# A state-space scan feeding a gated FFN: two sequences of the first scan, and w_in's first piece, ahead of the others

## The chip, the cores and the metric

The kernel runs on one core of one Trainium2 chip. The metric is the device time of one execution in microseconds; of the kernel before, six runs are given by their median, lowest and highest. A profile is one profiled execution; its rows are in microseconds from the start of its span unless marked ns. The engines are PE (TensorE matmul) with PEld (its weight loads), DVE (VectorE), ACT (ScalarE), POOL (GpSimd) and SP (SyncE, which here only issues DMAs).

## The reference

Four sequences of 768 positions with 8 heads go through a chunked state-space scan; its output, as 3072 tokens of 256, goes through `h @ w_in`, a gate with a cosine, and `@ w_out` (256 to 2048 and back).

```python
for c in range(nc):                        # chunks of 32
    cum = np.cumsum(la, axis=-1)           # la = log(clip(a))
    L = np.exp(cum[..., :, None] - cum[..., None, :]) * causal
    M = np.einsum('bhin,bhjn->bhij', Cc, Bc) * L
    y[:, :, sl] = M @ xc + (Cc @ state) * exp(cum)
    state = decay_full * state + sum(Bx)
h = x @ w_in;  g = h * np.cos(h);  out = g @ w_out
```

The weights arrive as 64-bit floats; x, a, B and C are 32-bit.

## The kernel before

The kernel takes six chunks of 128 positions (NC = 6) of all four sequences (NB = 4). For each chunk it makes yT (the scan's output, transposed, 512 tokens), and then 16 steps of the FFN (NF = 16, `n` counts them over all chunks). Step n is `first(n)`: four matmuls hp = w_in x yT, an integer copy k on ScalarE and w = hp/2pi - k on VectorE; `gate(n)`: the sine on ScalarE; `gated(n)`: gT = hp x w on VectorE; and, two steps later (LAG = 2), `second(n - 2)`: o += gT x w_out. In the first chunk the steps alternate between the halves of the tokens: even n takes sequences 0 and 1, odd n sequences 2 and 3 (`turn_of`), so hp(0) needs yT of the first two sequences only.

The order of each engine's instructions is the order in which the program writes them: there is a manual schedule, and each engine takes its own in turn. What the first chunk does for sequence b:

- `spread_a(b)` (L294): matmuls that spread a into PSUM (a_ps); `decays0(b)` (L303): a scan on VectorE over it (L309), then a copy and a memset on GpSimd (L312, L313), which give lam, the decays within halves of 64.
- `cross(b)` (L315): one matmul (L318) for two sequences, the product of the decays between the halves; two ScalarE copies put it into lam (L321), and `weigh` (L324) scales B by it on GpSimd, for the state (sc).
- `turn(b)` (L354): two TensorE transposes of B and C (L360), and three ScalarE copies to cT and bT.
- `intra(b)` (L369): four matmuls g = B x C (L374), and two VectorE products m = g x lam (L381).
- `finish(b)` (L385): eight matmuls y = m x x (L391), and a ScalarE copy into yT (L395). With `fills=1` it first issues a matmul of ones (L101), whose product isn't used.
- `first_scan` (L720): finish(3), then the 16 matmuls of the state's sums (s_ps, L478).

A weight piece (256 columns of w_in or 256 rows of w_out; 8 of each) comes as 64-bit words and is made 32-bit in pieces. `grade` (L178): ScalarE takes the high words' magnitude (L193), GpSimd clips it (L194), ScalarE scales the low words (L191); with `later=True` the L191 is returned as a function that the caller runs later. `join` (L201): VectorE shifts and merges bits (L207, L209), GpSimd adds the low words and writes the piece (L217). hp(0) and hp(1) use w_in's first piece, hp(2) and hp(3) its second; the second matmuls of steps 0 and 1 use w_out's first.

PSUM is given out in rings of two: tag "h" (hp, and before it a_ps and tp), tag "o" (o, and before it the warm-up, l_ps and y), tag "scan" (pairs of banks: g, tp, s_ps). A tile waits until the readers of the one two places before it in its ring are done. The same holds for the rings of SBUF tiles (m has four).

The SP queue issues the loads in the order in which the program writes them: `load(0, b)` for each sequence (B, C, x), with w_in's first piece ahead of the fourth sequence (L219 to L222), then a as rows (L223), five weight pieces, and, behind the writes of a_cut and a_all to DRAM (L691), the rest of the weights and the loads of chunk 1 (`rest_of_loads`).

Of the kernel before, what the change touches and what calls it, by code (L numbers as in the profile page):

```python
# [25 lines left out]
def kernel(  # L26
# [59 lines left out]
    def bank(shape, name, tag):  # L86
        return psum.tile(shape, FP32, tag=tag, bufs=2, name=name)

    def pair(name):

        return psum.tile([P, 2, 4 * P], FP32, tag="scan", bufs=2, name=name)
# [86 lines left out]
    def grade(which, i, later=False, n=1):  # L178

        t = words.pop((which, i), None)
        if t is None:
            return
        mag = conv.tile([P, 2 * WC], FP32, tag="mag", bufs=3, name="mag")
        last = conv.tile([P, 2 * WC], U32, tag="last", bufs=3, name="last")
        low, high, mags, lasts = (shares(which, ap, n) for ap in (t[:, :, 0], t[:, :, 1], mag, last))
        held[which, i] = list(zip(high, shares(which, mag.bitcast(U32), n), lasts))

        def rest(e=0):  # L190
            ACT.activation(lasts[e], low[e], AF.Copy, scale=2.0 ** -29)  # L191
        for e in range(n):
            ACT.activation(mags[e], high[e].bitcast(FP32), AF.Abs)  # L193
            G.tensor_scalar(out=mags[e], in0=mags[e], scalar1=MOST, scalar2=LEAST,  # L194
                            op0=ALU.min, op1=ALU.max)
            if not later:
                rest(e)
        if later:
            return rest
# [17 lines left out]
            G.tensor_tensor(out=dst.bitcast(U32), in0=bits, in1=last, op=ALU.add)  # L217

    for b in range(NB):  # L219
        if b == NB - 1:  # L220
            fetch("in", 0)
        load(0, (b, b + 1))  # L222
    nc.sync.dma_start(  # L223
# [70 lines left out]
    def spread_a(b, tag):  # L294


        spread[b] = ps = bank([P, H, W], "a_ps", tag)
        for t in range(2):
            PE.matmul(ps[t * W:(t + 1) * W], lhsT=those[:, b:b + 1].to_broadcast([P, W]),  # L299
                      rhs=a0s[:, t], start=True, stop=True, tile_position=(0, t * W),  # L300
                      skip_group_check=True)

    def decays0(b):  # L303

        lam[0, b] = l = scan.tile([P, 2, H, W], FP32, tag="lam", bufs=4, name="lam")
        flat = "p h i -> p (h i)"
        V.tensor_tensor_scan(out=l[:, 0].rearrange(flat), data0=spread.pop(b).rearrange(flat),  # L309
                             data1=unit0.rearrange(flat), initial=0.0,  # L310
                             op0=ALU.mult, op1=ALU.add)
        G.tensor_copy(out=l[W:P, 1], in_=l[W:P, 0])  # L312
        G.memset(l[W:P, 0], 0.0)  # L313

    def cross(b, tag):  # L315

        ps = bank([P, H, W], "l_ps", tag)
        PE.matmul(ps, lhsT=fros[:, b:b + 2].rearrange("p b j -> p (b j)"), rhs=tos,  # L318
                  start=True, stop=True)
        for t in range(2):  # L320
            ACT.copy(out=lam[0, b + t][0:W, 1], in_=ps[t * W:(t + 1) * W])  # L321
            weigh(0, b + t)

    def weigh(c, b):  # L324

        scaled[c, b] = sc = scan.tile([P, H, N], FP32, tag="sc", bufs=NB, name="sc")
        l = lam[c, b][:, :, P - 1:P] if c > 0 else lam[c, b][:, 1, :, W - 1:W]
        G.tensor_tensor(out=sc, in0=raw[c][0][:, 0, heads(b)],  # L328
                        in1=l.to_broadcast([P, H, N]), op=ALU.mult)
# [21 lines left out]
            return  # L351
        weigh(c, b)

    def turn(b, tag=None):  # L354

        bc = raw[0][0]
        tp = (pair("tp")[:, 0] if tag is None else bank([P, 4 * P], "tp", tag)
              ).rearrange("p (k i) -> p k i", k=4)
        for k in range(2):
            PE.transpose(tp[:, k], bc[:, k, heads(b)].rearrange("p h n -> p (h n)"), ident)  # L360

        cT = scan.tile([P, 2, P], FP32, tag="cT", name="cT")
        for t in range(2):
            ACT.activation(cT[:, t], tp[:, 1], AF.Copy, scale=slot[:, t:t + 1])
        bT = scan.tile([P, P], FP32, tag="bT", name="bT")
        ACT.copy(out=bT, in_=tp[:, 0])
        part[0, b] = (bT, cT)

    def intra(b):  # L369
        bT, cT = part[0, b]  # L370
        g = [pair("g") for _ in range(2)]
        for q in range(4):
            r = slice(32 * q, 32 * q + 32)
            PE.matmul(g[q // 2][:, q % 2, 0:2 * P], lhsT=bT[r],  # L374
                      rhs=cT[r].rearrange("p t (s i) -> p s t i", s=2), start=True, stop=True)
        l = lam.pop((0, b))
        m = scan.tile([P, 2, H, W], FP32, tag="m", bufs=4, name="m")
        for q in range(2):
            of = [t[:, :, q * HH:(q + 1) * HH].rearrange("p s (k t) i -> p k s (t i)", k=2)
                  for t in (m, l)]  # L380
            V.tensor_tensor(out=of[0], in0=g[q][:, :, 0:2 * P].rearrange(  # L381
                "p k (s i) -> p k s i", s=2), in1=of[1], op=ALU.mult)
        part[0, b] = m
# [122 lines left out]
        c, f = divmod(n, NF)  # L506
        return (f % 2, f // 2) if c == 0 else divmod(f, NJ)

    def first(n):
        c, f = divmod(n, NF)  # L510
        hp[n] = bank([P, TB], "hp", "h")

        u, j = turn_of(n)
        to_ = hp[n].rearrange("p (e t s i) -> p e t s i", e=2, t=2, s=2)
        y = yT[c].rearrange("p k (u s t i) -> p k u t s i", u=2, s=2, t=2)
        for e in range(2):
            fs = slice((2 * j + e) * P, (2 * j + e + 1) * P)
            for k in range(KT):
                PE.matmul(to_[:, e], lhsT=w_in[:, k, fs], rhs=y[:, k, u],  # L519
                          start=(k == 0), stop=(k == KT - 1), skip_group_check=True)  # L520

        k = ffn.tile([P, TB], I32, tag="k", name="k")
        ACT.activation(k, hp[n], AF.Copy, bias=0.25, scale=INV_2PI)  # L523
        turns[n] = w = ffn.tile([P, TB], FP32, tag="w", name="w")
        V.scalar_tensor_tensor(out=w, in0=hp[n], scalar=INV_2PI, in1=k,  # L525
                               op0=ALU.mult, op1=ALU.subtract)
# [137 lines left out]
    warm = bank([P, 4, P], "warm", "o")  # L664
    fill(warm, 2)
    spread_a(0, "h")
    turn(0)
    spread_a(1, "h")
    spread_a(2, "o")
    spread_a(3, "h")  # L670
    for b in range(NB):
        decays0(b)
    turn(1, "h")
    cross(0, "o")
    intra(0)
    turn(2, "h")
    cross(2, "o")
    intra(1)
    finish(0, "o")
    grade("in", 0, n=2)  # L680
    intra(2)
    turn(3, "h")
    finish(1, "o", 1)

    la = const.tile([RB, NU, P], FP32, name="la")
    cut = const.tile([RB, NU, P], FP32, name="cut")
# [4 lines left out]
        nc.sync.dma_start(  # L691
            out=dst.rearrange("(u b) h (c p) -> (b h c) u p", u=NU, p=P), in_=src)

    join("in", 0)
    finish(2, "o")
    intra(3)
    grade("in", 1)
    rest = grade("out", 0, later=True)
    join("in", 1)


    piece = {n: ("in", (n + 3) // 2) if n % 2 else ("out", n // 2) for n in range(NF)}
# [16 lines left out]

    def first_scan():  # L720

        finish(3, "o")
        for u in range(2):
            sums[u] = pair("s_ps")[:, :, 0:2 * D]
            for t in range(2):
                sum_up(0, 2 * u + t, sums[u][:, t])
# [25 lines left out]
    def ends(n):  # L752
        return [(c, us) for c, at, us, _, _, end in plan if at + end == n]

    rest_of_loads()
    for n in range(NC * NF + LAG):
        c, f = divmod(n, NF)
        if n < NC * NF:
            if f == 0 and c > 0:
                load(c + 2)  # L760
            first(n)
            if n == 0:
                first_scan()
            for at in pairs(n):
                turn2(*at)
            rests = [rest] if n == 0 else []
            if n + 1 in piece:
                rests.append(grade(*piece[n + 1], later=True))
            gate(n)
            for rest in rests:  # L770
                if rest:
                    rest()
            if n in piece:
                join(*piece[n])

            behind = [lambda at=at: halved(*at) for at in halves_at(n)]
            behind = [lambda at=(c, 2 * u + 1): masked(*at) for c, u in pairs(n - 2)] + behind
            if n not in piece and behind:
                behind.pop(0)()
            gated(n)  # L780
            for do in behind:
                do()
            if n in (1, 2):
                carry(0, n - 1, sums[n - 1])
        for i, js in differ_at.get(n, ()):
            differ_w(i, js)
        if n >= LAG:
            second(n - LAG)
        for c, u in pairs(n - 1):
            intra2(c, u)  # L790
            masked(c, 2 * u)
        for c, us in ends(n):
            finish2(c, us)
            if 1 in us:
                raw.pop(c)
        for c, u in pairs(n + 1):
            for b in (2 * u, 2 * u + 1):
                reaches(c, b)
                load_along(c + 1, (b,))
# [30 lines left out]
```

## Time and profile before

| what | us |
|---|---|
| median of 6 runs (lowest, highest) | 382.77 (382.22, 383.33) |
| the profiled execution, its own time | 382.64 |
| its span | 380.8 |
| TensorE busy / weight loads busy | 374.0 / 330.6 |
| VectorE / GpSimd / ScalarE busy | 279.8 / 213.0 / 172.6 |
| granted TensorE clock | 1.00 |

How to read it: the page of a profile gives busy times, the span in 40 slices, the chain of work that ended last, and groups of instructions; a group's row is line, engine, operation, out<-in with the shapes and the count, then busy time and mean ns, then the idle time of the engine just before it and what ended that. The timeline merges neighbouring instructions of one kind into a row of start, duration, engine, line, operation and count; a matmul of 32-bit data is two passes, so four matmuls of hp are x8. Two VectorE or ScalarE instructions in a row overlap by some 0.1 us. Shares of DMA over the first stretches: 0.99 from 4 to 10 us, 1.01 from 10 to 14, 0.95 from 14 to 18, 1.00 from 18 to 21.5, 1.08 from 21.5 to 25, 0.92 from 25 to 60.

### The profile page before, as it was taken

How to read it: one execution, taken by the hardware profiler on the slowest of the kernel's cores; microseconds unless marked ns; L12 is line 12 of the kernel's file. 1: busy time of each engine (PE TensorE's matmuls, PEld its weight loads, DVE VectorE, ACT ScalarE, POOL GpSimd, SP SyncE). 2: the span in 40 equal slices, each digit the busy share in tenths (PEclk: the TensorE clock that was granted, in tenths of full speed). 3: DMA queues.
4: the chain of work that ended last, by engine and by line, in shares of the span. 5: the costliest groups of instructions: out<-in, count | busy, mean ns of one | idle time of the engine just before them, and what ended most of it. 6: DMA issues, size and time to landing. Idle time of an engine off the chain costs nothing.

```text
span 380.8 us, 7676 instructions
## 1 busy us (share of the span) xinstructions
PE 374.0 (98%) x2980; PEld 330.6 (87%) x2980; DVE 279.8 (73%) x431; ACT 172.6 (45%) x303; POOL 213.0 (56%) x330
## 2 busy tenths in 40 slices
PE   8989999999999999999999999999999999999995
PEld 2568888889989899998899998899998999999995
DVE  8898999789699748877648976756976862644643
ACT  3887666544334433443434453424444433433441
POOL 5776555479863436773544683543585343454451
PEclk9999999999999999999999999999999999999999
DMA  7989999859322861420941340100100100000101
GB/s 86 261 238 279 248 223 138 151 88 171 90 87 77 111 60 58 134 75 2 109 46 55 83 116 10 43 2 2 28 3 3 28 2 2 12 17 0 29 0 28
DMA packets 106371, 30.41 MB, mean 80 GB/s; under 512 B 75521, under 2 KB 102241, under 8 KB 106337
## 3 DMA queue, kind: packets, MB, share of 16 engines
q1 hardware_dynamic: 106176, 29.81, 39.3%
q8 instruction: 23, 0.38, 0.4%
q10 hardware_dynamic: 160, 0.13, 0.1%
q14 instruction: 12, 0.09, 0.1%
HBM read 26.59 MB, written 3.34 MB: 79 GB/s over the span
## 4 chain that ended last, share of the span: by engine, by line
PE 96%; DVE 2%; POOL 0%; issue 0%; POOLq 0%
PE hp L519 44%; PE o L616 33%; PE o L578 7%; PE g L423 3%; PE y L457 3%; PE y L450 1%; PE tp L406 1%; PE a_ps L299 1%; PE warm L101 1%; DVE mag L209 1%; PE g L374 1%; DVE mag L207 1%; PE o L655 1%; PE s_ps L478 0%; PE l_ps L318 0%; PE tp L360 0%
## 5 line engine op out<-in xcount | busy, mean ns | idle before, releaser
L519 PE MATMUL hp<-yT,w_in 128*128 128x256 f32 x768 | 184.0, 382 | 1.7 <-DVE gT L535 1.3
L519 PEld LDWEIGHTS hp<-yT,w_in 128*128 128x128 f32 x768 | 139.4, 190 | 22.8 <-issue 4.9
L560 POOL TENSOR_TENSOR gd<-gT 128x256 f32<-128x256 f32 x79 | 59.4, 752 | 103.4 <-DVE gT L535 74.3
L530 ACT ACTIVATE w<-w,quarter 128x512 f32<-128x512 f32 x96 | 69.3, 722 | 84.4 <-DVE w L525 84.4
L525 DVE SCALAR_TENSOR_TENSOR w<-hp,k 128x512 f32<-128x512 f32 x96 | 65.6, 684 | 53.0 <-ACT k L523 52.9
L523 ACT ACTIVATE k<-hp 128x512 int32<-128x512 f32 x96 | 57.1, 595 | 98.3 <-PE hp L519 98.3
L535 DVE TENSOR_TENSOR gT<-hp,w 128x512 f32<-128x512 f32 x96 | 65.1, 678 | 30.6 <-ACT w L530 28.0
L616 PE MATMUL o<-words,gd 128*128 128x128 f32 x474 | 66.9, 277 | 0.0
L616 PEld LDWEIGHTS o<-words,gd 128*128 128x128 f32 x474 | 59.8, 192 | 0.5
L345 DVE TENSOR_TENSOR_SCAN lam<-arow,unit 128x512 f32<-128x512 f32 x40 | 55.8, 1395 | 0.0
L616 PEld LDWEIGHTS o<-w_out,gT 128*128 128x128 f32 x316 | 46.9, 191 | 3.6
L563 POOL TENSOR_TENSOR gd<-gT,gd 128x128 f32<-128x128 f32 x79 | 46.0, 583 | 6.2
L616 PE MATMUL o<-w_out,gT 128*128 128x128 f32 x316 | 48.0, 274 | 0.0
L562 POOL TENSOR_TENSOR gd<-gT,gd 128x128 f32<-128x128 f32 x79 | 42.7, 540 | 6.2
L616 PE MATMUL o<-w_out,gd 128*128 128x128 f32 x158 | 30.6, 275 | 0.0
L616 PE MATMUL o<-words,gT 128*128 128x128 f32 x158 | 30.6, 275 | 0.0
L578 PE MATMUL o<-w_out,gT 128*128 128x256 f32 x128 | 30.2, 379 | 0.0
L578 PEld LDWEIGHTS o<-w_out,gT 128*128 128x128 f32 x128 | 24.2, 190 | 3.3
L436 DVE TENSOR_TENSOR m<-g,lam 128x512 f32<-128x512 f32 x40 | 25.6, 680 | 0.0
L616 PEld LDWEIGHTS o<-words,gT 128*128 128x128 f32 x158 | 24.0, 192 | 0.0
L616 PEld LDWEIGHTS o<-w_out,gd 128*128 128x128 f32 x158 | 24.0, 192 | 0.0
L328 POOL TENSOR_TENSOR sc<-bc,lam 128x128 f32<-128x128 f32 x20 | 8.3, 417 | 14.4 <-DVE lam L345 7.3
(91 smaller groups left out, 291.4 us busy)
## 6 DMA issues: line engine op xcount, KB each, us to landing
arow<-a_cut SPq DMA_DIRECT2D x20, 512.0 KB, 3.9
words<-in_moe_w_in_dram SPq DMA_DIRECT2D x8, 512.0 KB, 6.0
words<-in_moe_w_out_dram SPq DMA_DIRECT2D x8, 512.0 KB, 8.8
out_dram<-sum SPq DMA_DIRECT2D x18, 128.0 KB, 2.5
xr<-in_x_dram SPq DMA_DIRECT2D x4, 512.0 KB
along<-a_all SPq DMA_DIRECT2D x20, 64.0 KB
xr<-in_x_dram SPq DMA_DIRECT2D x8, 128.0 KB
bc<-in_B_dram SPq DMA_DIRECT2D x4, 256.0 KB, 5.1
```

The source lines that it names most:

```text
L345: V.tensor_tensor_scan(out=lam[c, b][:, hs].rearrange("p h i -> p (h i)"), data0=rows_.rearrange("p h i -> p (h i)"), data1=unit.rearrange ...
L436: V.tensor_tensor(out=of[0], in0=g[q][:, :, s * 2 * P:(s + 1) * 2 * P], in1=of[1], op=ALU.mult)
L519: PE.matmul(to_[:, e], lhsT=w_in[:, k, fs], rhs=y[:, k, u], start=(k == 0), stop=(k == KT - 1), skip_group_check=True)
L523: ACT.activation(k, hp[n], AF.Copy, bias=0.25, scale=INV_2PI)
L525: V.scalar_tensor_tensor(out=w, in0=hp[n], scalar=INV_2PI, in1=k, op0=ALU.mult, op1=ALU.subtract)
L530: ACT.activation(cos, cos, AF.Sin, bias=quarter, scale=TWO_PI)
L535: V.tensor_tensor(out=gT[n], in0=hp.pop(n), in1=cos, op=ALU.mult)
L560: G.tensor_tensor(out=d[:, 0:2], in0=g[:, 1:2].to_broadcast([P, 2, P]), in1=g[:, 3::-3], op=ALU.subtract)
L562: G.tensor_tensor(out=d[:, 2], in0=g[:, 0], in1=d[:, 0], op=ALU.subtract)
L563: G.tensor_tensor(out=d[:, 3], in0=g[:, 2], in1=d[:, 2], op=ALU.subtract)
L578: PE.matmul(o[c, u][:, t], lhsT=g[:, 2 * e + t], rhs=w_out[:, 2 * j + e], start=(j == e == t == 0), stop=(j == NJ - 1 and e == 1), skip_gr ...
L616: PE.matmul(at[q], lhsT=a_[q], rhs=w[q], start=(j == 0 and q in starts), stop=(j == NJ - 1), skip_group_check=True)
```

## The change

Only the start of the kernel changes, up to the end of step 0, and with it the places of a few steps in the queues.

- On SP, w_in's first piece is fetched ahead of the third sequence instead of the fourth.
- The first two sequences are scanned first: cross(0), intra(0), turn(1), grade of w_in's first piece, then the third's a, decays and intra(1), cross(2), the fourth's a. `decays0(3)` is split: its tile is allocated early, so that cross(2)'s copies can write it, and its scan comes behind the join of w_in's first piece. finish(0) and finish(1) follow each other; the filling matmul is gone.
- `weigh` is no longer part of `cross`: those of sequences 0 and 1 come behind a_cut and a_all on GpSimd, those of 2 and 3 in `start`.
- hp(0) is issued before sequences 2 and 3 are finished: its first half, then the turn of the fourth sequence, then its second half, then intra(3), and only then step 0's k and w; finish(2) and finish(3) follow, then gate(0).
- The ScalarE work on the low words (L191) of w_in's second piece, w_out's first and w_in's third comes behind gate(0) in a row; the joins of w_in's second and w_out's first piece surround gated(0). Before, the L191 of w_in's second piece followed its L193 directly.
- The sums of the state (s_ps) come behind hp(1) instead of ahead of it.
- The tiles of `turn` are half as large (two of 128 columns) and come from tags "h" and "o".

```diff
     for b in range(NB):
-        if b == NB - 1:
+        if b == 2:
             fetch("in", 0)
         load(0, (b, b + 1))
...
-    def decays0(b):
+    def decays0(b, early=False):
...
+        if early:
+            lam[0, b] = scan.tile([P, 2, H, W], FP32, tag="lam", bufs=4, name="lam")
+            return
...
     def cross(b, tag):
...
-        for t in range(2):
-            ACT.copy(out=lam[0, b + t][0:W, 1], in_=ps[t * W:(t + 1) * W])
-            weigh(0, b + t)
+        crosses.update({b + t: ps[t * W:(t + 1) * W] for t in range(2)})
+
+    def crossed(b):
+        ACT.copy(out=lam[0, b][0:W, 1], in_=crosses.pop(b))
...
-    def first(n):
+    def first(n, between=None):
...
         for e in range(2):
+            if e and between:
+                between()
...
+        if not between:
+            turned(n)
+
+    def turned(n):
...
     spread_a(0, "h")
-    turn(0)
+    turn(0, pair("tp")[:, 0, 0:2 * P])
     spread_a(1, "h")
+    decays0(0)
+    decays0(1)
+    cross(0, "o")
+    crossed(0)
+    crossed(1)
+    intra(0)
+    turn(1, bank([P, 2 * P], "tp", "h"))
+    grade("in", 0, n=2)
     spread_a(2, "o")
+    decays0(2)
+    intra(1)
+    cross(2, "o")
     spread_a(3, "h")
-    for b in range(NB):
-        decays0(b)
-    turn(1, "h")
-    cross(0, "o")
-    intra(0)
-    turn(2, "h")
-    cross(2, "o")
-    intra(1)
+    decays0(3, early=True)
+    crossed(2)
+    crossed(3)
     finish(0, "o")
-    grade("in", 0, n=2)
+    finish(1, "o")
+    join("in", 0)
+    decays0(3)
+    turn(2, bank([P, 2 * P], "tp", "h"))
     intra(2)
-    turn(3, "h")
-    finish(1, "o", 1)
...
-    join("in", 0)
-    finish(2, "o")
-    intra(3)
-    grade("in", 1)
-    rest = grade("out", 0, later=True)
-    join("in", 1)
+    weigh(0, 0)
+    weigh(0, 1)
...
     def first_scan():
 
-        finish(3, "o")
...
+    def start():
+
+        first(0, lambda: turn(3, bank([P, 2 * P], "tp", "o")))
+        intra(3)
+        turned(0)
+        later = [grade("in", 1, later=True)]
+        finish(2, "o")
+        for b in range(NB):
+            if b > 1:
+                weigh(0, b)
+            del lam[0, b]
+        finish(3, "o")
+        later.append(grade("out", 0, later=True))
+        gate(0)
+        for do in (*later, grade(*piece[1], later=True)):
+            if do:
+                do()
+        join("in", 1)
+        gated(0)
+        join("out", 0)
+
     rest_of_loads()
+    start()
...
+            if n == 0:
+                continue
             first(n)
-            if n == 0:
+            if n == 1:
                 first_scan()
```

More of the change, by code (lines that the diff above doesn't have):

```diff
@@ L301, in spread_a @@
                       skip_group_check=True)
-    def decays0(b):
-        lam[0, b] = l = scan.tile([P, 2, H, W], FP32, tag="lam", bufs=4, name="lam")
+    def decays0(b, early=False):
+        if early:
+            lam[0, b] = scan.tile([P, 2, H, W], FP32, tag="lam", bufs=4, name="lam")
+            return
+        if (0, b) not in lam:
+            decays0(b, True)
+        l = lam[0, b]
         flat = "p h i -> p (h i)"
@@ L313, in decays0 @@
         G.memset(l[W:P, 0], 0.0)
+    crosses = {}
     def cross(b, tag):
@@ L352, in decays, with turn @@
         weigh(c, b)
-    def turn(b, tag=None):
+    def turn(b, tp):
         bc = raw[0][0]
-        tp = (pair("tp")[:, 0] if tag is None else bank([P, 4 * P], "tp", tag)
-              ).rearrange("p (k i) -> p k i", k=4)
+        tp = tp.rearrange("p (k i) -> p k i", k=2)
         for k in range(2):
@@ L375, in intra @@
                       rhs=cT[r].rearrange("p t (s i) -> p s t i", s=2), start=True, stop=True)
-        l = lam.pop((0, b))
+        l = lam[0, b]
         m = scan.tile([P, 2, H, W], FP32, tag="m", bufs=4, name="m")
@@ L765 @@
                 turn2(*at)
-            rests = [rest] if n == 0 else []
-            if n + 1 in piece:
-                rests.append(grade(*piece[n + 1], later=True))
+            rests = [grade(*piece[n + 1], later=True)] if n + 1 in piece else []
             gate(n)
```

## The prediction

> **What bounds the kernel now.** I read first the page's chain of work, then the idle times of TensorE's groups, then its timeline over the first 32 us, and last the timelines of ScalarE, VectorE and GpSimd over the same stretch.
>
> ```profile
> PE 96%; DVE 2%; POOL 0%; issue 0%; POOLq 0%
> ...
> L519 PE MATMUL hp<-yT,w_in 128*128 128x256 f32 x768 | 184.0, 382 | 1.7 <-DVE gT L535 1.3
> ```
>
> TensorE ends the kernel. Its largest group waited 1.7 us in all, 1.3 of them once, for a gT. Where that was, the timeline tells:
>
> ```profile
> 18.18 2.29 PE L519 MATMUL hp<-yT,w_in 128*128 128x256 f32 x8 [0.31 <-POOL w_in L217]
> 20.40 0.64 PE L391 MATMUL y<-m,xr 128*32 128x128 f32 x16
> 20.86 0.63 PE L478 MATMUL s_ps<-xr,sc 128*32 128x64 f32 x32
> 21.54 1.99 PE L519 MATMUL hp<-yT,w_in 128*128 128x256 f32 x8
> 24.87 1.97 PE L519 MATMUL hp<-yT,w_in 128*128 128x256 f32 x8 [1.34 <-DVE gT L535]
> 26.68 1.89 PE L578 MATMUL o<-w_out,gT 128*128 128x256 f32 x8
> ```
>
> hp(0) starts at 18.18, hp(1) at 21.54, hp(2) at 24.87; from there no row of TensorE shows idle time, and the table of stretches gives it 35.00 of 35.00 us between 25 and 60. What follows hp(2) is the same work before and after the change. So the whole question is **when hp(2) starts**: later or earlier by d, the kernel ends later or earlier by d, unless a new wait follows.
>
> hp(2) needs three things: its PSUM bank (gT(0) of VectorE), w_in's second piece (the sum at L217 on GpSimd), and TensorE free. The rows that prepare that piece:
>
> ```profile
> 18.51 0.68 ACT L191 ACTIVATE last<-words 128x512 uint32<-128x512 uint32 x1
> ...
> 21.12 0.37 ACT L395 COPY yT<-y 128x256 f32<-128x256 f32 x1
> 21.38 0.68 ACT L193 ACTIVATE mag<-words 128x512 f32<-128x512 f32 x1
> 22.10 0.72 ACT L530 ACTIVATE w<-w,quarter 128x512 f32<-128x512 f32 x1
> 22.73 1.25 ACT L191 ACTIVATE last<-words 128x512 uint32<-128x512 uint32 x2
> ```
>
> ```profile
> 20.48 0.98 DVE L209 SCALAR_TENSOR_TENSOR mag<-words,mag 128x512 uint32<-128x512 uint32 x1
> 21.39 0.68 DVE L525 SCALAR_TENSOR_TENSOR w<-hp,k 128x512 f32<-128x512 f32 x1
> 21.99 1.12 DVE L207 TENSOR_SCALAR mag<-mag 128x512 uint32<-128x512 uint32 x1
> ```
>
> ```profile
> 21.55 1.28 POOL L217 TENSOR_TENSOR w_in<-mag,last 128x512 uint32<-128x512 uint32 x1 [0.63 <-DVE mag L209]
> 22.79 0.79 POOL L194 TENSOR_SCALAR mag<-mag 128x512 f32<-128x512 f32 x1
> ```
>
> Before, the low words of that piece are ready at 19.19 (the L191 at 18.51) and the piece at 22.83, two us ahead of hp(2). Only gT(0) is late.
>
> **What the Trainium skill says.** "SBUF — State Buffer", section "Who interferes with whom": VectorE and GpSimd share a port pair under an exclusive lock; a VectorE instruction in a two-port mode, or with two SBUF inputs, and a GpSimd instruction that reads SBUF exclude each other for the whole instruction. The trace agrees: L207 of 21.99 ends 0.29 after GpSimd's L217 lets go (22.82), and took 1.12 where an undisturbed one takes 0.41; L209 of 20.48 ends 0.55 after GpSimd's L194 ends (20.92). "TensorE: Matmul & The Clock Gate", section "What's actually happening": full clock needs sustained work, and an idle window of about 3.4 us halves it. Here a 64-row pass of a_ps took 0.9 us at 4.8 and 0.43 from 6.6 on, and the gap of 1.34 us left hp(2) at full speed; longer gaps the trace doesn't show.
>
> **The change part by part.** I worked out the start of each instruction in the new order as the later of its engine's last issue and its last input, with the durations above and those of the same rows elsewhere in the first 25 us, and the lock. The same rule on the old order puts hp(2) at 24.60 where the trace has 24.87, so it is good to some 0.3 us.
>
> *Sequences 0 and 1 ahead.* The first cross product follows a_ps(1): 7.50 instead of 9.59. The decays' copies end at 9.74, m(0) at 10.67 (was 12.75), m(1) at 13.05 (was 14.66), with the third scan (1.22) between them on VectorE. y(1) takes the bank of the second cross product, so it waits for its two copies (0.58 each), to 13.61; yT(1) is done at 14.67.
>
> *w_in's first piece ahead of sequence 2 on SP.* Landings of before are 10.27 for sequence 2's x and 12.26 for the piece, so the piece takes 2.0 and now lands near 10.25; sequence 2's loads land 2.0 later, 11.0 to 12.3. Their first user (the turn of 2) comes at 14.05, which hides it with 2.4 to spare; without that cover it would cost up to 2.0. The piece is joined at 15.7 (was 19.29).
>
> *hp(0).* The turn of 2 is at 14.05, its ScalarE copies (0.80) stand behind yT(1), g(2) is at 15.53, hp(0)'s first half at 16.2, the turn of 3 at 17.2, hp(0) done at 18.7 instead of 20.47. That is 1.8 us won.
>
> *But hp(1) needs sequences 2 and 3.* The turn of 3 lies inside hp(0); its copies end at 18.45, g(3) at 19.24, m(3) (0.2 of hand-over, 0.61 + 0.69) at 20.72, y(3) at 21.21, yT(3) runs 21.25 to 21.62. Before it ran 21.12 to 21.49. So hp(1) starts at 21.68 against 21.54: **the gain is gone** already. The four s_ps (0.62) now stand behind hp(1) and end at 24.04.
>
> *The low words of w_in's second piece move.* This edit decides. ScalarE's L191 for that piece, at 18.51 before, now stands behind gate(0), that is behind yT(3), the high words of w_out's first piece, the sine, and the high words of w_in's third: 21.25 + 0.27 + 0.57 + 0.63 + 0.57 = 23.29, done 23.97. Three L191 in a row follow each other there, with k(1) queued behind (25.0; was 23.89). On GpSimd the joining sum (L217) also stands behind L194 of w_in's third piece, which waits for ScalarE until 23.49. Then the lock: L207 of w_out's first piece (from 23.46, behind gT(0)) holds it to 23.87, L194 ends 0.47 later at 24.34, L209, waiting since 23.90, holds it to 24.88, and L217 ends 1.14 later, at **26.02**. hp(2) starts at **26.07**.
>
> *The rest.* Four L328 moved later end at 21.4, before s_ps needs them (23.4). The filler of 0.53 removed from y(1)'s bank lies where TensorE would now wait anyway. a_cut and a_all are issued some 1.3 later (before: 16.67 and 17.36), and the SP queue behind them too (w_out's third piece, chunk 1's loads): before, a_cut landed only at 23.89, behind weight pieces that keep the DMA engines at 1.0 of their time from 18 to 25, so this lies in that queue; uncovered it would be 1.3 on loads whose users come 4 us later or more. Allocating the fourth decays early and the smaller tp tiles: the same instructions, 0.
>
> *What is late next.* hp(3) needs gT(1). k(1) 25.0, w at 25.65, L207 waits for w_out's sum (1.28 behind 26.02: 27.27) until 27.55, L194 to 28.02, L209 to 28.57, gT(1) 29.18, usable 29.31; hp(3) is due at 26.07 + 3.46 = 29.53. That holds by 0.2.
>
> **Sum.** 26.07 - 24.87 = +1.20 us. On the profiled execution, 382.64 (span 380.8 and 1.8 around it), that is 383.84; its time is 0.13 below the median of 382.77, so in medians **384.0**. Unknown from both sides: who gets the lock. If L217 goes before L209, hp(2) is at 25.73 (+0.86); if L194 also goes before L207 (they are 0.03 apart), 25.57 (+0.70). If the rule is as early here as on the old order, +1.47.
>
> **The rivals.** 0.2% (0.77 us) is about what a measurement of this kernel can tell from no change.
> *A, forecast:* as summed, 383.6 to 384.4.
> *B, the same wait with a kinder lock:* 382.77 + 0.70 to 0.86, 383.5 to 383.6. For it: the two requests are 0.03 apart. Against: L209 is queued 0.4 ahead of L217.
> *C, faster:* the piece isn't last. Then hp(2) starts when s_ps ends, at 24.04: -0.83, 381.9. It decides from L217 ending before 24.8; it would need yT(3) at 20.0 instead of 21.25, for instance if ScalarE's copies of the fourth turn didn't wait for hp(0)'s first half. For it: hp(0) is indeed 1.8 earlier. Against: four engines in series give 21.25.
> *D, worse:* TensorE's gap (now 2.0 behind s_ps, after smaller ones) halves its clock for a window of 3.4 us, +1.7, or hp(3) waits for gT(1) too: 384.8 or more.
> *E, no effect:* pieces cancel or the order doesn't bind as read: 382.8.
>
> **How the numbers follow.** A 0.58, B 0.15, C 0.11, D 0.08, E 0.08. Slower by over 0.2%: A, D and half of B, 0.73; within: half of B and E, 0.16; faster: C, 0.11. The range 382.9 to 384.8 holds A, B, half of D and some of E, 8 in 10.
>
> **What would show it.** hp(0) near 16.2 and done by 18.8; hp(1) within 0.3 of 21.6; L191 of w_in's second piece near 23.3; hp(2) released by L217, not by gT; no idle row after it. If hp(2) is released by gT or by nothing, or yT(3) comes before 20.5, I am wrong.

## The result and the profile after

| | before | after |
|---|---|---|
| median of the runs made together (lowest, highest, how many) | 382.63 (381.83, 383.46, 39) | 384.18 (383.64, 386.82, 18) |
| ratio of times | | 1.0053, 95% interval 1.0040 to 1.0065 |
| the profiled execution, its own time / span | 382.64 / 380.8 | 386.51 / 384.6 |
| second a_ps starts | 6.59 | 7.05 |
| hp(0), hp(1) | 18.18, 21.54 | 17.09, 22.55 |
| hp(2), hp(3) | 24.87, 28.40 | 26.94, 32.18 |

The change makes the kernel slower: by 0.53% in the ratio of the means, from 382.63 to 384.18 in medians, against a forecast of 384.0. The second a_ps is the spread of the second sequence's a. The lines below are of the kernel after. There L367 and L373 are the old L360 and L366 (a turn and its last copy), L381 the old L374 (g), L388 the old L381 (m), L398 and L402 the old L391 and L395 (y and yT), L485 the old L478 (s_ps), L528 the old L519 (hp), L536, L543 and L548 the old L523, L530 and L535 (k, the sine, gT) and L591 the old L578 (o); the joins and grades keep their lines. First TensorE's timeline (start, duration, then the row; in brackets the idle time before it and what ended that):

```profile
16.45 0.71 PE L381 MATMUL g<-cT,bT 32*128 32x256 f32 x8 [0.93 <-ACT bT L373]
17.09 1.13 PE L528 MATMUL hp<-yT,w_in 128*128 128x256 f32 x4
18.06 0.38 PE L367 MATMUL tp<-ident,bc 128*128 128x128 f32 x2
18.28 1.03 PE L528 MATMUL hp<-yT,w_in 128*128 128x256 f32 x4
...
21.63 0.42 PE L398 MATMUL y<-m,xr 128*32 128x128 f32 x8 [0.17 <-DVE m L388]
22.55 1.99 PE L528 MATMUL hp<-yT,w_in 128*128 128x256 f32 x8 [0.49 <-ACT yT L402]
24.47 0.65 PE L485 MATMUL s_ps<-xr,sc 128*32 128x64 f32 x32
26.94 3.56 PE L528 MATMUL hp<-yT,w_in 128*128 128x256 f32 x8 [1.81 <-POOL w_in L217]
30.29 2.05 PE L591 MATMUL o<-w_out,gT 128*128 128x256 f32 x8
32.18 1.89 PE L528 MATMUL hp<-yT,w_in 128*128 128x256 f32 x8
```

hp(0) is early, hp(1) is not, and hp(2) stands 1.81 us behind L217, the sum of w_in's second piece. No row behind it shows idle time, to the end. The other three engines, in order ScalarE, VectorE, GpSimd:

```profile
23.59 0.67 ACT L193 ACTIVATE mag<-words 128x512 f32<-128x512 f32 x1
24.14 1.84 ACT L191 ACTIVATE last<-words 128x512 uint32<-128x512 uint32 x3
```

```profile
23.72 0.69 DVE L548 TENSOR_TENSOR gT<-hp,w 128x512 f32<-128x512 f32 x1 [0.49 <-ACT w L543]
24.33 0.42 DVE L207 TENSOR_SCALAR mag<-mag 128x512 uint32<-128x512 uint32 x1
24.78 0.98 DVE L209 SCALAR_TENSOR_TENSOR mag<-words,mag 128x512 uint32<-128x512 uint32 x1
```

```profile
24.34 0.88 POOL L194 TENSOR_SCALAR mag<-mag 128x512 f32<-128x512 f32 x1 [0.56 <-ACT mag L193]
25.19 1.70 POOL L217 TENSOR_TENSOR w_in<-mag,last 128x512 uint32<-128x512 uint32 x1
```

That is the chain that was forecast, link by link: L207 and L194 start together, L194 takes 0.88 instead of 0.61, L209 has the port until 25.76, and L217 takes 1.70 instead of 1.28. The times are not those forecast: hp(1) was to start within 0.3 of 21.6 and starts at 22.55.

One thing stands beside it. hp(2) took 3.56 where it took 1.97 before. The table of stretches of the kernel after (the stretch and its length, the busy time and the instructions of PE, PEld, DVE, ACT and POOL, then the clock granted to TensorE, DMA share, GB/s):

```profile
23.80:27.20 3.40, 1.59 (x37) 1.07 (x36) 2.63 (x5) 2.95 (x6) 2.86 (x3) 1.00 0.70 126
27.20:30.60 3.40, 3.40 (x9) 2.67 (x9) 2.98 (x4) 1.64 (x4) 2.77 (x3) 0.50 0.88 264
30.60:34.00 3.40, 3.40 (x17) 2.96 (x17) 2.80 (x5) 2.41 (x4) 1.75 (x3) 1.00 1.04 395
```

After 3.4 us in which TensorE was busy for 1.59, its clock was 0.50 for 3.4 us: half of that, 1.7 us, was lost. (hp(3) starts 5.24 behind hp(2); with the low words back, below, at full clock, 3.56.) This was the rival D, and it comes and goes: of the nineteen executions of this kernel, the profiled one among them, five have a mean clock of 0.996 and took 386.51 to 386.82; the other fourteen have 0.998 to 1.000 and took 383.64 to 384.73 (their middle: 383.96).

So the 3.87 us between the two profiled executions are: 0.46 from the first 7 us, whose work is the same (the second a_ps starts at 7.05 instead of 6.59); **1.61 at hp(2)**, counted from the second a_ps (26.94 - 7.05 = 19.89 against 24.87 - 6.59 = 18.28); 1.71 from the half clock; 0.1 is left over. The 0.46 is luck of the execution: TensorE's clock rises at 6.72 here and at 5.70 in the other, so the second half of a_ps(0) runs at half clock here and at full clock there, as their rows show, after first, before second.

```profile
5.68 1.07 PE L299 MATMUL a_ps<-a0s,those 128*64 128x512 f32 x2
```

```profile
5.68 0.61 PE L299 MATMUL a_ps<-a0s,those 128*64 128x512 f32 x2
```

Every kernel here has that luck: in the twelve profiled executions the second a_ps starts between 6.12 and 7.11. (The 39 runs of before spread over 1.6 us; how much of that is this luck, their times alone don't tell.) So I compare traces from the second a_ps on:

| kernel | hp(1) | hp(2) | waits of TensorE from hp(2) on | hp(95) | median (lowest, highest, runs) | ratio to before |
|---|---|---|---|---|---|---|
| before | 14.95 | 18.28 | hp(2) 1.34, gT | 363.37 | 382.63 | 1 |
| after | 15.50 | 19.89 | hp(2) 1.81, w_in | 364.96, with 1.71 taken off for the half clock | 384.18 (383.64, 386.82, 18) | 1.0053 (1.0040, 1.0065) |
| low words back | 15.50 | 19.88 | hp(2) 1.81, w_in | 365.01 | 383.91 (383.52, 384.48, 7) | 1.0028 (1.0016, 1.0039) |
| and sum ahead | 15.50 | 18.03 | o(0) 0.72, w_out | 364.39 | 384.00 (383.07, 384.33, 10) | 1.0030 (1.0019, 1.0041) |
| gap filled | 15.50 | 19.90 | none | 365.03 | 384.72 (384.32, 384.92, 6) | 1.0047 (1.0036, 1.0059) |
| another piece | 15.51 | 18.02 | o(0) 1.14, w_out | 364.79 | 384.13 (383.38, 384.61, 9) | 1.0032 (1.0019, 1.0045) |
| longer gap | 15.50 | 22.05 | hp(2) 3.98, w_in | 369.50, with two windows of half clock in it | 387.84 (387.71, 389.52, 5) | 1.0146 (1.0126, 1.0165) |
| no lock | 15.50 | 19.20 | hp(2) 1.12, w_in; o(0) 1.49, w_out | 366.06 | 385.88 (385.81, 385.95, 2) | 1.0084 (1.0066, 1.0103) |
| turn early | 15.35 | 19.73 | hp(2) 1.81, w_in | 364.84 | 384.14 (383.31, 386.53, 3) | 1.0051 (1.0019, 1.0083) |
| scan between | 14.97 | 19.38 | hp(2) 1.82, w_in | 364.52 | 385.23 (383.09, 385.58, 8) | 1.0050 (1.0029, 1.0070) |
| mended | 15.35 | 17.86 | o(0) 0.72, w_out | 363.94 | 383.25 (382.54, 383.83, 13) | 1.0016 (1.0008, 1.0024) |
| mended more | 15.14 | 17.65 | o(0) 0.61, w_out | 363.67 | 382.37 (381.49, 383.03, 20) | 0.9988 (0.9980, 0.9997) |

hp(1), hp(2) and hp(95), the last one, are starts in us behind the second a_ps in the profiled execution. A ratio is that of the means, to the runs of before made together with the kernel's own; their medians lie between 382.56 and 382.82.

### The profile page after: what moved, and what is told of

Read it like the earlier page. It is cut to its first block, busy times and chain, and to the rows that moved or that the text cites. A ratio compares the mean times of both kernels' runs of the same rounds, so it can differ in the third digit from the quotient of the medians.

```text
span 384.6 us, 7678 instructions
## 1 busy us (share of the span) xinstructions
PE 375.7 (98%) x2978; PEld 330.8 (86%) x2978; DVE 279.8 (73%) x431; ACT 172.4 (45%) x303; POOL 212.7 (55%) x330
## 4 chain that ended last, share of the span: by engine, by line
PE 96%; ACT 1%; POOL 1%; DVE 0%; issue 0%; DVEq 0%; POOLq 0%; ACTq 0%
PE hp L528 44%; PE o L629 32%; PE o L591 7%; PE g L430 3%; PE y L464 2%; PE y L457 1%; PE tp L413 1%; PE a_ps L299 1%; PE warm L101 1%; PE g L381 1%; PE l_ps L325 1%; PE o L668 0%; ACT cT L371 0%; PE s_ps L485 0%; POOL w_in L217 0%; PE y L398 0%
## 5 line engine op out<-in xcount | busy, mean ns | idle before, releaser
L528 PE MATMUL hp<-yT,w_in 128*128 128x256 f32 x768 | 185.5, 385 | 2.3 <-POOL w_in L217 1.8
L528 PEld LDWEIGHTS hp<-yT,w_in 128*128 128x128 f32 x768 | 140.3, 191 | 23.2 <-issue 3.5
L543 ACT ACTIVATE w<-w,quarter 128x512 f32<-128x512 f32 x96 | 69.3, 722 | 84.0 <-DVE w L538 84.0
L536 ACT ACTIVATE k<-hp 128x512 int32<-128x512 f32 x96 | 57.0, 594 | 99.5 <-PE hp L528 99.4
L548 DVE TENSOR_TENSOR gT<-hp,w 128x512 f32<-128x512 f32 x96 | 65.1, 678 | 31.1 <-ACT w L543 28.5
L591 PE MATMUL o<-w_out,gT 128*128 128x256 f32 x128 | 30.4, 380 | 0.0
L591 PEld LDWEIGHTS o<-w_out,gT 128*128 128x128 f32 x128 | 24.5, 192 | 3.4
L194 POOL TENSOR_SCALAR mag<-mag 128x512 f32<-128x512 f32 (+1 forms) x17 | 12.6, 744 | 9.4 <-ACT mag L193 9.3
```

Source lines behind the costliest of these rows:

```text
L528: PE.matmul(to_[:, e], lhsT=w_in[:, k, fs], rhs=y[:, k, u], start=(k == 0), stop=(k == KT - 1), skip_group_check=True)
L543: ACT.activation(cos, cos, AF.Sin, bias=quarter, scale=TWO_PI)
L548: V.tensor_tensor(out=gT[n], in0=hp.pop(n), in1=cos, op=ALU.mult)
L591: PE.matmul(o[c, u][:, t], lhsT=g[:, 2 * e + t], rhs=w_out[:, 2 * j + e], start=(j == e == t == 0), stop=(j == NJ - 1 and e == 1), skip_gr ...
```

## What decides hp(2): low words, order of the sums, or the lock

My theory was that the low words' move decides: L191 of w_in's second piece behind the sine. The rival: the place of the joining sum behind GpSimd's clip of the third piece, and the port's lock. Four edits of the kernel after. The first puts the low words back:

```diff
-        later = [grade("in", 1, later=True)]
+        grade("in", 1)
+        later = []
```

> One part of the change undone: the low words of w_in's second piece (L191) directly behind its high words, as before the change; the sum (L217) stays where the change put it. Theory 1, mine in full (the L191 was one of two things; L217 also stands behind L194 of w_in's third piece and then behind VectorE's L209): L217 still issues near 25.2 us and ends near 26.9, hp(2) stays within 0.15 us of the changed kernel's, the median within 0.3 of it. Theory 2 (the L191 alone decides, as my text put it): hp(2) 0.3 to 1.8 us earlier, the median likewise.

```profile
19.59 0.68 ACT L191 ACTIVATE last<-words 128x512 uint32<-128x512 uint32 x1
```

```profile
23.52 0.89 POOL L194 TENSOR_SCALAR mag<-mag 128x512 f32<-128x512 f32 x1 [0.55 <-ACT mag L193]
24.37 1.70 POOL L217 TENSOR_TENSOR w_in<-mag,last 128x512 uint32<-128x512 uint32 x1
26.03 1.46 POOL L217 TENSOR_TENSOR w_out<-mag,last 128x512 uint32<-128x512 uint32 x1
```

The low words are ready at 20.27, four us ahead of L217, and L217 ends where it did: hp(2) is at 19.88, after 19.89. What stands in front of L217 is L194 of the third piece, which waits for ScalarE's L193. **The low words alone decide nothing.** The median is 0.27 below that of the change; but none of its seven runs lost the 1.7 us, and hp(95) is level (365.01 and 364.96). That the low words would never matter isn't shown: in the kernel after they are ready at 24.82 (the first of the three L191), only 0.37 ahead of L217, and no run moves the sum ahead while they stay late.

The second edit also puts the sum ahead of the third piece's clip:

```diff
         gate(0)
+        join("in", 1)
         for do in (*later, grade(*piece[1], later=True)):
...
-        join("in", 1)
         gated(0)
```

> As the run before, and the sum of w_in's second piece (L217) ahead of L194 of w_in's third piece. Theory 1: L217 runs from 23.8 to 25.1 us, hp(2) is released by TensorE's own s_ps or gT(0) near 25.1 instead of 26.9; then o(0) waits for w_out's first piece until about 27.9 (due at 26.9), so that 0.8 to 0.9 of the 1.8 is left: the median 0.8 to 1.0 below a run of the changed kernel at full clock, about 382.9, and 0.2 to 0.5 above the kernel before. Rival (the scan's own order costs the time): hp(2) and the median within 0.3 of the changed kernel.

```profile
23.57 1.29 POOL L217 TENSOR_TENSOR w_in<-mag,last 128x512 uint32<-128x512 uint32 x1
24.83 0.79 POOL L194 TENSOR_SCALAR mag<-mag 128x512 f32<-128x512 f32 x1
26.31 1.27 POOL L217 TENSOR_TENSOR w_out<-mag,last 128x512 uint32<-128x512 uint32 x1 [0.69 <-ACT mag L193]
```

```profile
24.91 1.99 PE L528 MATMUL hp<-yT,w_in 128*128 128x256 f32 x8
27.63 1.99 PE L591 MATMUL o<-w_out,gT 128*128 128x256 f32 x8 [0.72 <-POOL w_out L217]
```

Now L217 goes first and undisturbed (1.29), and hp(2) starts behind s_ps without a wait, 1.86 earlier. But w_out's first piece is next in line: o(0) waits 0.72 for its L217, and of the 1.86 only 0.6 are left at hp(95). That is less than the 0.8 to 0.9 expected, and the median, 384.00, doesn't show it beside the 383.96 of the change without the half clock.

The third edit lets hp(2) and hp(3) read w_in's first piece, so the second need not be there (these two steps are then computed with other weights):

```diff
-            fs = slice((2 * j + e) * P, (2 * j + e + 1) * P)
+            jw = 0 if n in (2, 3) else j
+            fs = slice((2 * jw + e) * P, (2 * jw + e + 1) * P)
```

> The changed kernel, but hp(2) and hp(3) take the columns of w_in's first piece instead of the second's: part of the product is computed with other weights, all instructions stay. That removes the wait of hp(2) for L217 and nothing else. Theory 1: hp(2) starts when s_ps ends, near 25.1 us, and then o(0) waits for w_out's first piece, which ends near 28.1: o(0) some 0.5 earlier than in the changed kernel (28.7 at full clock), the median 383.2 at full clock. Rival (the piece is not what hp(2) lacks): hp(2) near 26.9 as before. A third outcome, o(0) not held: the median near 381.9.

```profile
24.94 1.99 PE L529 MATMUL hp<-yT,w_in 128*128 128x256 f32 x8
28.07 1.99 PE L592 MATMUL o<-w_out,gT 128*128 128x256 f32 x8 [1.14 <-POOL w_out L217]
```

hp(2) is at 18.02 without a wait, as with the sum ahead: so w_in's piece, and nothing else, held it. o(0) then waits 1.14 for w_out's piece, whose sum here still stands behind a locked L217, and 0.2 of the 1.87 are left at hp(95). The gain of a step that no longer waits was nearly all taken by the next piece.

The fourth takes L207 and L209 of w_out's first piece out of L217's way, by joining that piece one step later:

```diff
         gated(0)
-        join("out", 0)
...
             if n == 1:
+                join("out", 0)
                 first_scan()
```

> The changed kernel, but VectorE's and GpSimd's join of w_out's first piece behind w of step 1 instead of behind gT(0), so that no L207 or L209 asks for the shared port when the sum (L217) of w_in's second piece is due. Theory 1 (the lock lengthens L217 from 1.28 to 1.70, and L194 before it from 0.61 to 0.88): L217 takes 1.28, and hp(2) starts 0.4 to 0.7 earlier after a_ps(1) than in the changed kernel; o(0) then waits for w_out's first piece, so the time is no better, 0.3 to 1.0 above. Rival (no lock; GpSimd is slow there by itself): L217 stays at 1.7 and hp(2) where it was.

```profile
24.38 0.61 POOL L194 TENSOR_SCALAR mag<-mag 128x512 f32<-128x512 f32 x1 [0.56 <-ACT mag L193]
24.98 1.27 POOL L217 TENSOR_TENSOR w_in<-mag,last 128x512 uint32<-128x512 uint32 x1
```

```profile
26.31 1.99 PE L528 MATMUL hp<-yT,w_in 128*128 128x256 f32 x8 [1.12 <-POOL w_in L217]
29.80 1.56 PE L591 MATMUL o<-w_out,gT 128*128 128x256 f32 x6 [1.49 <-POOL w_out L217]
```

(The view ends at 31 us, within that o(0).) L194 is back at 0.61 and L217 at 1.27, and hp(2) starts 0.69 earlier (19.20): that is the 0.27 and 0.43 that the two were longer. **That is the lock's share.** The other 1.12 of the wait is the place in the queue: with the sum ahead it is gone. The piece that was put off costs more than that: o(0) waits 1.49, and hp(95) is 1.1 later than after. The two runs are 1.9 above the change without the half clock, where 0.3 to 1.0 was expected; the trace accounts for 1.1 of that.

## The half clock

If TensorE's idle time in front of hp(2) halves the clock, then filling it must prevent that, and more of it must bring it about every time. Filled with two more warm-up matmuls (x4 in the profile) behind s_ps:

```diff
                 sum_up(0, 2 * u + t, sums[u][:, t])
+        fill(bank([P, 4, P], "warm", "o"), 2)
```

> The changed kernel with two matmuls of ones behind s_ps, into a bank of their own, where TensorE waits 1.8 us for w_in's second piece. Theory 1: the runs of the changed kernel above 384 us (a granted clock of 0.996 to 0.999, and 0.5 for 3.4 us behind that gap in its profile) are the gap's doing: with it filled the clock reads 1.000 in all runs, all lie within 1 us, and the median is 383.7, the lowest unchanged; hp(2) starts when it did. Rival (the clock falls whatever TensorE does there, for example with the start's phase): the same share of runs at 386.7 remains.

```profile
24.54 0.65 PE L485 MATMUL s_ps<-xr,sc 128*32 128x64 f32 x32
25.12 1.98 PE L101 MATMUL warm<-ones 128*128 128x512 f32 x4
27.01 1.99 PE L528 MATMUL hp<-yT,w_in 128*128 128x256 f32 x8
```

hp(2) is where it was (19.90) and takes 1.99; none of the six runs was above 384.92. The median is a miss all the same: 384.72 instead of 383.7, and the lowest is 384.32 instead of the change's 383.64. From the second a_ps the trace is level with that of the low words put back (365.03 and 365.01), but its second a_ps starts at 7.11 and theirs at 6.24, so in this one execution the difference is the luck of the first 7 us; whether it is in the other five, their times don't tell. The mean clock was 0.998 to 0.999, not the 1.000 I expected, but the trace has the whole of that at its very end, where the clock drops with TensorE done. Six runs against five in nineteen are weak by themselves; the other direction is stronger:

```diff
+        for _ in range(7):
+            G.memset(a_in, 0.0)
         join("in", 1)
```

> The changed kernel with seven memsets on GpSimd ahead of the sum (L217) of w_in's second piece, so that TensorE's gap ahead of hp(2) grows from 1.8 to about 3.5 us. Theory 1 (the clock falls when more than about half of one of the windows of 3.41 us that the records show lies in a gap): now every run has such a window, the clock reads 0.997 or less in all runs, and the median is 1.7 of wait plus 0.7 to 1.7 of slow clock above the undisturbed runs of the changed kernel (383.9): 386.3 to 387.4. Rival (the fall has nothing to do with the gap): median 385.6, with the slow clock in a quarter of the runs, as in the changed kernel.

```profile
29.05 2.50 PE L528 MATMUL hp<-yT,w_in 128*128 128x256 f32 x5 [3.98 <-POOL w_in L217]
```

```profile
23.60:27.00 3.40, 1.48 (x37) 0.93 (x35) 2.59 (x4) 2.79 (x6) 2.56 (x8) 1.00 0.64 102
27.00:30.40 3.40, 1.35 (x3) 1.17 (x4) 3.37 (x3) 1.37 (x3) 3.34 (x5) 0.50 0.86 253
30.40:33.80 3.40, 3.40 (x9) 2.68 (x9) 2.05 (x4) 1.40 (x3) 1.68 (x2) 0.50 1.02 384
33.80:37.20 3.40, 3.40 (x17) 2.96 (x17) 2.50 (x5) 1.85 (x4) 2.15 (x2) 1.00 1.02 204
```

(The view of the first row ends at 31 us.) With a gap of 3.98 all five runs had it: three with a clock of 0.996 and 387.7 to 387.8, two with 0.989 and 0.991 and 389.4 to 389.5, the profiled one with two windows at 0.50, one for each stretch of 3.4 us that was less than half busy. The median, 387.84, is above the 386.3 to 387.4 expected: the gap came out longer than the 3.5 it was meant to be, and two runs had a second window. So the gap makes the half clock.

Which executions with a gap of 1.8 get it, the traces tell in part. In each of them the times at which the clock changes lie whole multiples of 3.413 us behind its first rise (after: 6.72, 27.20, 30.61). With the low words put back the clock rises at 4.99, so that a border of these windows, 25.47, falls into the gap (24.31 to 26.12): the two windows that share the gap are busy for 2.26 and 2.76, and the clock stays full. In the kernel after the whole gap lies in one window, 23.79 to 27.20. So it matters where the gap lies among the windows. But that isn't all: the kernel with the scan between (below) got the half clock in six of eight runs, and its profiled execution did not, though the window that held its gap was busy for 1.59, as after.

## Where hp(0)'s lead is lost, and a version that keeps more of it

hp(0) came early but g(2) in front of it waited 0.93 for ScalarE's copies of the third sequence's turn, queued behind yT(0) and yT(1). Moving that turn ahead of finish(0) should bring sequences 2 and 3 forward:

```diff
     crossed(2)
     crossed(3)
+    turn(2, bank([P, 2 * P], "tp", "h"))
     finish(0, "o")
...
-    turn(2, bank([P, 2 * P], "tp", "h"))
```

> The changed kernel with one edit: the turn of the third sequence ahead of y(0), so that its copies run while TensorE works and g(2) doesn't wait 0.93 us for them. Theory 1 (hp(2) hangs on yT(3) through ScalarE's and GpSimd's queues): yT(3) 0.9 to 1.2 earlier, and hp(2) earlier by the same amount within 0.2, still released by L217; median about 1.0 below the undisturbed runs of the changed kernel, 382.9. Rival (hp(2) hangs on the weights' own work or their landing): yT(3) earlier, hp(2) by less than 0.4.

```profile
14.90 0.71 PE L381 MATMUL g<-cT,bT 32*128 32x256 f32 x8
16.43 1.10 PE L528 MATMUL hp<-yT,w_in 128*128 128x256 f32 x4 [0.81 <-DVE lam L314]
```

A miss: g(2)'s wait is gone, but hp(0) waits 0.81 in its place, and hp(1) gains 0.15. hp(0) takes the PSUM bank of a_ps(3), which VectorE's scan of the fourth sequence reads; that scan stands behind the join of w_in's first piece. If this is it, the scan has to go between the two halves of the join, which calls the function that it is given ahead of its second half (its own lines are left out here):

```diff
-    join("in", 0)
-    decays0(3)
+    join("in", 0, lambda: decays0(3))
```

> The turn of 2 ahead of the y of 0 and 1, as in the kernel with that edit alone, and besides the fourth sequence's scan on VectorE between the two halves of the join of w_in's first piece instead of behind both. There hp(0) waited 0.81 for that scan, whose PSUM bank it takes. If the scan is what kept the early turn from paying: the scan starts about 14.2 instead of 15.3 and ends near 15.4, hp(0) starts within 0.2 of g(2)'s end, 0.6 to 0.8 earlier against the second a_ps, and the second half of it may wait up to 0.3 for the piece's second half (its sum ends near 17.3); yT(3) and hp(1) 0.4 to 0.7 earlier than 15.35 behind the second a_ps. hp(2) moves as much only as far as the low words and the lock let it: 0.3 to 0.6. If something else holds the fourth sequence (the copies on ScalarE, g(3), m(3)), hp(0) is earlier and hp(1) is not.

From here on lines behind the join stand two higher (L383 is the kernel after's L381, L530 its L528); L219 is its L217.

```profile
14.77 0.71 PE L383 MATMUL g<-cT,bT 32*128 32x256 f32 x8
15.41 1.13 PE L530 MATMUL hp<-yT,w_in 128*128 128x256 f32 x4
16.38 0.38 PE L369 MATMUL tp<-ident,bc 128*128 128x128 f32 x2
17.17 1.13 PE L530 MATMUL hp<-yT,w_in 128*128 128x256 f32 x4 [0.41 <-POOL w_in L219]
```

hp(0) starts right behind g(2), its second half waits 0.41 for the piece's second half, and hp(1) is 0.38 earlier than with the turn alone, just under the 0.4 to 0.7 expected; hp(2) 0.35 earlier. The scan was what held it. The median says nothing of this: six of the eight runs had the half clock.

Then all of it together. Mended: the early turn, the low words at once, the sum of w_in's second piece ahead of the third's clip, w_out's high words ahead of yT(3), and w_in's third piece joined behind gT(1). Mended more: the same with the scan between.

```diff
+    turn(2, bank([P, 2 * P], "tp", "h"))
     finish(0, "o")
...
-    turn(2, bank([P, 2 * P], "tp", "h"))
...
-        later = [grade("in", 1, later=True)]
+        grade("in", 1)
         finish(2, "o")
...
+        rests = [grade("out", 0, later=True)]
         finish(3, "o")
-        later.append(grade("out", 0, later=True))
         gate(0)
-        for do in (*later, grade(*piece[1], later=True)):
+        join("in", 1)
+        rests.append(grade(*piece[1], later=True))
+        for do in rests:
             if do:
                 do()
-        join("in", 1)
...
-            if n in piece:
+            if n in piece and n != 1:
                 join(*piece[n])
...
             gated(n)
+            if n == 1:
+                join(*piece[n])
```

> The new scan with its weights put right: the turn of the third sequence ahead of y(0), the low words of w_in's second piece at once, its sum ahead of L194 of the third piece, w_out's high words ahead of yT(3), and gT(1) ahead of the join of w_in's third piece. Theory 1 (the scan's order does win time, and the places of the weights' steps gave it back): hp(1) about 1.1 earlier than in the changed kernel, hp(2) near 23.6 to 24.1 in a run whose second a_ps starts at 6.6 (before: 24.87), hp(3) near 27.2 (28.40); median 0.8 to 1.4 below the kernel before, 381.2 to 381.8. Rival (VectorE, busy at 0.95 of its time in that stretch, or the DMA sets the pace): hp(3) not before 28.2, median within 0.4 of the kernel before.

383.25: better than the change, but not the 381.2 to 381.8 expected; the ratio to before is 1.0016 (1.0008 to 1.0024). hp(2) is 0.42 earlier than before at last, and there is no wait left in front of it; but o(0) waits 0.72 for w_out's first piece, so that hp(95) ends up 0.57 later than before.

> The mended order (turn of 2 early; low words of w_in's second piece at once; that piece summed ahead of the high words of w_in's third) with the fourth's scan between the two halves of the join of w_in's first piece. Leaves nothing out. If the scan was what was late: hp(1) 0.4 to 0.7 earlier than 15.35 behind the second a_ps, hp(2) up to 0.5 earlier than 17.86, o(0) still waiting for w_out's first piece for 0.5 to 0.8; the time 0.3 to 0.6 below the mended order's 383.25, that is 382.7 to 382.9: level with the kernel before (382.57) within 0.2%, not faster. If w_out's first piece is bound by something that does not move with it, the wait at o(0) grows by what hp(2) gains and the time stays at 383.2.

```profile
21.26 1.99 PE L530 MATMUL hp<-yT,w_in 128*128 128x256 f32 x8 [0.49 <-ACT yT L404]
23.19 0.65 PE L487 MATMUL s_ps<-xr,sc 128*32 128x64 f32 x32
23.77 1.99 PE L530 MATMUL hp<-yT,w_in 128*128 128x256 f32 x8
26.38 1.99 PE L593 MATMUL o<-w_out,gT 128*128 128x256 f32 x8 [0.61 <-POOL w_out L219]
```

382.37, a ratio of 0.9988 (0.9980 to 0.9997) to before: the best of all, but within the 0.2% that I count as no change, and the trace does not show where it would be faster (hp(95) is 0.30 later than before, from the second a_ps). I take it as level. The bound is now w_out's first piece.

## Why the prediction was right, and where its working was not

- *hp(0) early, 1.8 won; "the gain is gone" at hp(1).* Right in the mechanism. From the second a_ps hp(0) is done 1.62 earlier than before (12.26 against 13.88). Forecast and measured from there: hp(0) 9.6 and 10.04, yT(3) 14.66 and 15.07, hp(1) 15.09 and 15.50. The turn of the fourth sequence, its g, m and y, and yT(3) in series take what hp(0) won, as it said. But its own sign, hp(1) within 0.3 of 21.6, was missed: 22.55, and 22.09 without the luck of 0.46.
- *"This edit decides" (the low words).* Wrong. The kernel with the low words back is at 19.88 against 19.89. What decides is the other half of the same paragraph: L217 behind L194 of the third piece, and the lock. The end of L217 was found as the latest of several inputs, and the sentence gave the credit to one that was not the latest, in its own sum either (23.97 against 24.34).
- *The lock: L194 to end 0.47 after L207, L217 1.14 after L209.* Right: 0.47 (25.22 against 24.75) and 1.13 (26.89 against 25.76). Without the contention hp(2) is 0.69 earlier.
- *The sum, +1.20 at hp(2).* Too small by 0.41: 1.61. The mis-sized term, as far as rows can tell, is TensorE's spacing in the first steps. I took starts of a_ps 0.91 apart, l_ps to g 0.95, from before's rows, where like steps stand together. After, in an order of unlike steps, a_ps to l_ps and a_ps to y take 1.01 and l_ps to g 1.05:

```profile
7.05 1.08 PE L299 MATMUL a_ps<-a0s,those 128*64 128x512 f32 x4
8.06 1.13 PE L325 MATMUL l_ps<-both,fros 128*128 128x512 f32 x2
9.11 0.71 PE L381 MATMUL g<-cT,bT 32*128 32x256 f32 x8
```

  The lag behind the forecast is 0.10 at the first l_ps, 0.57 at the turn of the third sequence (forecast 7.46, measured 8.03), and 0.41 to 0.46 at g(2), hp(0), yT(3), hp(1) and the end of L217; up to that turn no row of TensorE shows idle time. Neighbouring steps here use TensorE's array in different tilings (the 128\*64, 128\*128 and 32\*128 of the rows). The Trainium skill, "TensorEngine Tiling (Array Packing)", section "Key Properties", says that changing the tiling mode drains TensorE; it gives no price. Rows of before fit: l_ps behind tp, both 128\*128, took 1.02; behind a_ps it takes 1.13 above. That is a comparison of rows; no run here took the tilings apart, so the drain as the cause is not shown. I had allowed for +1.47 at most, for another reason.
- *hp(3) held by 0.2.* Right: hp(3) did not wait. gT(1) was done at 30.02; at full clock hp(3) would have been due near 30.50 (an estimate: 26.94 and the 3.56 of the kernel with the low words back). In that kernel it was done 1.03 ahead of hp(3) (28.65 against 29.68).
- *SP's queue past w_in's first piece and a_cut, at nothing.* Right: no wait for a load shows in the rows from 25 us on.
- *Rival D, 0.08.* It came in five of nineteen executions, at the 1.7 us given. It was priced right and thought too rare, and it came on top of A, not in its place: I took "the gap of 1.34 us left hp(2) at full speed" for a sign that one of 2.0 would too.
- *The median.* 384.0 against 384.18 is nearer than the working deserves, and that is luck. The 0.41 and the half clock both came on top; but the median without the half clock is only 1.33 above before (383.96 - 382.63), not the 1.61 of the traces. The other 0.28 stays open; the luck of the first 7 us, which is in every run, moved single executions by more.

## What to carry to other kernels

When a step waits for the latest of several inputs, moving an earlier one shows nothing (the low words: 19.88 against 19.89) until all later ones are moved too; undo one at a time, and then look at who is next (here w_out's piece took most of what hp(2) gained). When short steps are reordered on TensorE, take their spacing from rows with the same neighbours. Where an edit opens a gap on TensorE, price a half-clock window beside the gap itself: here a gap of 1.8 brought one in some executions (5 of 19, none of 7, 1 of 3, 6 of 8 in the four kernels that have it), one of 3.98 in all five, and one of 1.34 in no run of before.

## What I had not expected of the hardware

- The clock halved after windows in which TensorE was still busy for 1.59 of 3.40 us. The Trainium skill, "TensorE: Matmul & The Clock Gate", section "What's actually happening", describes a free-running window of 3.413 us and an idle window as the condition; the length agrees (3.41 us at 0.50, 6.83 with the longer gap), and the idle window need not be wholly idle. The windows that a half clock followed were busy for 1.60, 1.49 and 1.36 (after, and the longer gap). None followed the windows with a gap that were busy for 1.83 or more, before's 2.07 among them, and none the one that was busy for 1.59 (the scan between). The exact condition stays open.
- A wait costs more than its idle time in the row. With the mended order o(0) shows 0.72 idle, yet starts 2.71 behind hp(2) instead of 1.83, and hp(3) comes 1.83 behind it instead of 1.73: 0.98 in all. The rows account for it: hp(2) lasts 1.99, so that o(0) without a wait starts 0.16 ahead of its end, and that overlap is lost too; and o(0) behind a gap lasts 1.99 instead of 1.89, another 0.10. Count from start to start, not the idle time.
